# Two cached attention blocks for one token: the order of the loads at both ends of the load queue, the place of the turning, and the bank of the second block's output sums

## The chip, the cores and the metric

The kernel runs on one core of a Trainium2 chip. The metric is the device time in microseconds of one execution; the time given for a kernel is the median of its runs. A trace of one profiled execution gives the durations, the waits and the transfers that are used below.

## The reference

Two independent blocks, A and B, each decode one token for two batch entries with 32 heads of width 192 over a cache of 8192 keys. Both have the same shapes here, and every tensor is bf16. The outputs (2, 1, 640) stand side by side.

```python
def _A_ref(x, k_cache, v_cache, wq, wo):           # _B_ref computes the same
    q = (x @ wq).reshape(B, Sq, Hq, Dh).transpose(0, 2, 1, 3)
    scores = jnp.einsum("bhqd,bhkd->bhqk", q, k) * (Dh ** -0.5)
    p = softmax(scores, axis=-1)
    o = jnp.einsum("bhqk,bhkd->bhqd", p, v)
    return o.transpose(0, 2, 1, 3).reshape(B, Sq, Hq * Dh) @ wo
out = jnp.concatenate([A, B], axis=-1)
```

x is (2, 1, 640), each cache (2, 32, 8192, 192), wq (640, 6144), wo (6144, 640). The caches are 805 of the 837 MB that are read.

## The kernel before, in words

**Units.** The work on the caches is cut into 64 units: a unit is one batch entry of a pair of heads (two batch entries, 16 pairs a block, two blocks). Units 0 to 31 are block A, 32 to 63 block B. "K63" is the K of unit 63, "V61" the V of unit 61. A unit's K or V is one load of 6.29 MB: the two heads lie on the two halves of the 128 partitions, with 128 keys of 192 numbers on each partition.

**One unit on the engines.** VectorE multiplies K by the unit's q, 32 keys a time (`dve_mul`, L280, four products a unit). TensorE sums each product over the 192 numbers by 12 matmuls with the identity (`pe_sum`, L352) into one of the four PSUM banks `scps`, and VectorE reduces the rest (`dve_red`, L283). The maximum goes over the partitions by POOL (L261), ScalarE makes the exponentials (`act_exp`, L317) and writes them into `pb`, the weights of the next matmuls. TensorE adds up their sum (`pe_l`, L358) and multiplies them with V (`pe_pv`, L365: 64 matmuls of 384 columns, two keys a partition in each). In `pb` each matmul has 34 columns: rows 0 and 1 of the result take the first of the two keys, rows 32 and 33 the second, and the 30 columns between are zero. VectorE and ScalarE add the two, divide by the sum and put the head's output into `qall` (L294 to L303).

**Start.** wq of both blocks is loaded whole; q is made by 80 matmuls a block (`pe_q`, L344), over an x that is spread over columns (`xbc`). The two wqs, x and `xbc` lie in `big`, the same SBUF tile that later holds the three buffers for K and V (`BUFE` each, 24576 numbers a partition) and two buffers for products. wq of A lies over buffers 0 and 1, x and `xbc` at the start of buffer 2, wq of B over the rest.

**End.** When all pairs of a block are done, the turning (`pe_turn`, L374, four matmuls a pair) brings the heads' outputs onto the partitions in the bank `oTps`, ScalarE copies them (`act_ot`, L324), and 96 matmuls a block multiply them with wo (`pe_out`, L387) and add into the bank `outps`. ScalarE evicts that (`act_out`, L327) and the output is stored. wo (7.86 MB a block) comes in eight pieces: A in two halves, B in pieces of 16, 16, 8, 4, 2 and 2 of its 48 rows. A row of wo here is 640 numbers on each of 128 partitions.

**Order.** All loads of wq, K, V and wo are issued by SP, in the order in which they are written (the loop of L468 and the one behind it), and each may carry a wait that holds everything behind it on SP. The loads of K and V are K0, K1, V0, K2, V1, and so on to K62, V61, K63, V62, V63; load i takes buffer i mod 3 and waits until load i - 3 has been used: a K by its last product, a V by its matmuls. In place of that, K0 and K1 wait for block A's q and V0 for block B's. wo piece 0 stands ahead of V63 and waits for K63's last product; the other pieces stand behind V63, which is loaded in three cuts.

On the engines each stream is put together from a table of slots, a slot a unit, sorted by an order number within the slot (`put`). In slot u TensorE does the sums of unit u, then the exponentials' sum and the V matmuls of unit u - 1. Slots 64 and 65 (`E1`, `E2`) hold the end: block A's turning, V63's matmuls, A's outputs, block B's turning, B's outputs. TensorE's stream runs as a loop over six slots wherever the slots look alike (`_find`), and is written out elsewhere.

The lines that matter most:

```python
    wq_off = [0, NBUF * BUFE + 2 * PRODE - WQE]
...
    loads = [("k", 0)]
    for u in range(1, NU):
        loads += [("k", u), ("v", u - 1)]
    loads.append(("v", LASTU))
...
        if i < 2:
            w = [("pq", PPB - 1)]
        elif i == 2:
            w = [("pq", NP - 1)]
        if (kind, u) == ("v", LASTU):
            S_sp.add(ld_wo(0), waits=pieces[0][4])
```

Of the kernel before, what the change touches and what calls it, by code (L numbers as in the profile page):

```python
# [6 lines left out]
ACTF = mybir.ActivationFunctionType  # L7
AXL = mybir.AxisListType
BF16 = mybir.dt.bfloat16
# [94 lines left out]
def build_kernel(nc, blocks, out):  # L104
# [4 lines left out]
    T = Sk // 64  # L109
# [12 lines left out]
    scale = float(Dh) ** -0.5  # L122
    NBUF = 3
    MP = 34
    QW = 2 * Dh
    BUFE = T * Dh
    PRODE = TC * Dh
# [3 lines left out]
    with ExitStack() as es:  # L131
# [34 lines left out]
        xoff = 2 * BUFE  # L166
        assert wq_off[0] + WQE <= xoff
        XBE = NBLK * DC * 128
        assert xoff + XBE + D <= wq_off[1]
        xbc = big[:, xoff:xoff + XBE].rearrange("p (k c m) -> p k c m", k=NBLK, c=DC)  # L170
        x4 = big[0:NBLK * B, xoff + XBE:xoff + XBE + D]

        reg = {}
        S_sp = _Stream("sp", sem("s_sp"), reg)
# [30 lines left out]
        bk, b62, b63 = buf["k", LASTU], buf["v", LASTU - 1], buf["v", LASTU]  # L205
        assert (bk, b62, b63) == (2, 0, 1)
        HWR = WR // 2
        woA = bk * BUFE
        pieces = [
            (0, 0, HWR, woA, [("m", LASTU, NCH - 1)]),  # L210
            (0, HWR, WR, woA + HWR * D, [("s", LASTU, NCH - 1)]),
            (1, 0, 16, b62 * BUFE, [("pv", LASTU - 1)]),
            (1, 16, 32, b62 * BUFE + 16 * D, []),
            (1, 32, 40, b63 * BUFE, [("pv", LASTU, 0)]),
            (1, 40, 44, b63 * BUFE + 8 * D, []),
            (1, 44, 46, b63 * BUFE + 12 * D, []),
            (1, 46, 48, b63 * BUFE + 14 * D, []),
        ]
        assert 16 * D <= BUFE // 2 and 32 * D <= BUFE and woA + WR * D <= NBUF * BUFE + 2 * PRODE
        for n in range(len(pieces)):  # L220
            dsem(("wo", n))

# [90 lines left out]
        def act_exp(u):  # L313
            def fn(eng):
                for s in range(2):
                    r = slice(64 * s, 64 * s + 64)
                    ins = eng.activation(pb[u % 2][r, :, s::32], sc[u % 2][r, :].rearrange("p (j a) -> p j a", a=2),  # L317
                                         ACTF.Exp, bias=nb[u % 2][r, :], scale=scale, accum_out=rs[u % 2][r, s:s + 1])
                return ins
            return fn  # L320
# [3 lines left out]
            return lambda eng: eng.activation(oTz[blk][:, :, 2:4], src, ACTF.Identity)  # L324

        def act_out(blk):
            return lambda eng: eng.activation(out_sb[blk][:], outps[0:4, 0:NH2], ACTF.Identity)  # L327

        def out_dma(blk, half):
            dst = out[:, 0, blk * D + half * NH2: blk * D + (half + 1) * NH2]  # L330
# [26 lines left out]
        def pe_l(u):  # L357
            return lambda eng: eng.matmul(ops[u % 2][0:2, QW:QW + 1], rs[u % 2][:], ones[:], start=True, stop=True)  # L358

        def pe_pv(u, j0, j1):  # L360
            vv = kv[buf["v", u]].rearrange("p (j a) d -> p j (a d)", a=2)

            def fn(eng):
                for j in range(j0, j1):
                    ins = eng.matmul(ops[u % 2][0:MP, 0:QW], pb[u % 2][:, j, :], vv[:, j, :],  # L365
                                     start=(j == 0), stop=(j == TJ - 1))
                return ins
            return fn
# [11 lines left out]
        def pe_out(n):  # L380
            blk, r0, r1, off, _ = pieces[n]
            wo = big[:, off:off + (r1 - r0) * D].rearrange("p (i n) -> p i n", n=D)

            def fn(eng):
                for i in range(r0, r1):
                    for half in range(2):
                        ins = eng.matmul(outps[0:4, 0:NH2], oTz[blk][:, i, 2 - 2 * half:6 - 2 * half],  # L387
                                         wo[:, i - r0, half * NH2:(half + 1) * NH2],
                                         start=(i == 0 and half == 0), stop=(i == WR - 1 and half == 1))
                return ins  # L390
            return fn
# [19 lines left out]
        for u in range(NU):  # L411
            for c in range(NCH):
                w = [("k", u), ("qa", u // B), ("qx", u // B), back("s", u, c, 2)]
                if u == 0:
                    w.append(("pq", NP - 1))
                put("dve", u, 2 + 2 * c, dve_mul(u, c), w, ("m", u, c))
                put("dve", u, 2 + 2 * min(c + 1, NCH - 1) + 1, dve_red(u, c),
                    [("s", u, c), key("mx", u - 2), key("exp", u - 2)], ("r", u, c))
                put("pe", u, 0, pe_sum(c),
                    [("m", u, c), back("r", u, c, NCH), ("id1",), ("qx", NP - 1), ("qa", NP - 1)], ("s", u, c), ("s", c))  # L420
            put("dve", u, 12, dve_max(u), [("r", u, NCH - 1), key("ar", u - 2), ("init",)], ("mx", u))
            put("pool", u, 0, pool_ar(u), [("mx", u), key("nb", u - 2)], ("ar", u))
            put("act", u, 0, act_nb(u), [("ar", u), key("exp", u - 2)], ("nb", u))
            put("act", u, 1, act_exp(u), [("nb", u), key("pv", u - 2), key("l", u - 2), ("init",)], ("exp", u))
            w0 = [("exp", u), key("os", u - 2), key("rc", u - 2), ("init",)]
            put("pe", u + 1, 2, pe_l(u), w0, ("l", u), ("l", u % 2))
            cuts = VCUT.get(u)
            if cuts is None:
                put("pe", u + 1, 3, pe_pv(u, 0, TJ), [("v", u)], ("pv", u), ("pv", u % 2, buf["v", u]))
            else:  # L430
                for c, (t0, t1) in enumerate(zip(cuts[:-1], cuts[1:])):
                    put("pe", u + 1, 3 + 0.01 * c, pe_pv(u, t0 // 2, t1 // 2), [("v", u, c)],
                        ("pv", u) if t1 == T else ("pv", u, c))
# [6 lines left out]
        for blk, slot, order in ((0, E1, 0), (1, E2, 0)):  # L440
            for hp in range(PPB * blk, PPB * (blk + 1)):
                lastp = hp == NP - 1
                put("pe", slot if not lastp else E2, order if not lastp else 5, pe_turn(hp),
                    [("of", B * hp + 1), ("place",)] + ([("ot", 0)] if blk else []), ("t", hp))
        put("act", E1, 2, act_ot(0), [("t", PPB - 1), ("init",)], ("ot", 0))
        put("act", E2, 8, act_ot(1), [("t", NP - 1), ("init",)], ("ot", 1))
        where = {0: (E1, 4), 1: (E2, 4)}
        for n, p in enumerate(pieces):
            slot, order = where.get(n, (E2, 6 + 0.01 * n))
            w = [("wo", n), ("ot", p[0])]  # L450
            if p[0] and n == 2:
                w.append(("oev", 0))
            put("pe", slot, order, pe_out(n), w, ("f", n))
# [121 lines left out]
```

## Time and profile before

| | before |
|---|---|
| median of three runs | 1964.46 us |
| the three runs | 1961.86, 1964.46, 1965.69 us |
| profiled execution, its own time | 1963.75 us |
| span of its trace, first to last instruction | 1962.0 us |
| granted TensorE clock, mean | 0.949 |
| busy: TensorE, VectorE, ScalarE, POOL | 78%, 57%, 8%, 2% |
| read from HBM | 836.77 MB |

The trace gives times in microseconds from the first instruction. PE is TensorE's matmuls, PEld its weight loads, DVE VectorE, ACT ScalarE, SPq the instructions by which SP issues loads. A row of the timeline has its start, its duration, the engine, the line of the kernel, the operation, its tiles and their shapes, how many were merged, and in brackets the idle time before it with what ended that. A row of the windows has the stretch, its length, then the busy time of PE, PEld, DVE, ACT and POOL with the number of instructions, the granted clock, the busy share of the 16 DMA engines and GB/s. A row of the loads has the tensor, the queue, the count, the size of one and the microseconds from its issue to its landing. A row of the chain of waits has its start, its duration and what it was. A matmul's own duration counts from its entry to its modelled end; neighbours overlap.

### The profile page before, as it was taken

The page shows a single profiled execution, that of the slowest core. Times are in us where ns is not written, and L with a number is a line of the kernel's source. Part 1 is how long each engine was busy: PE and PEld are TensorE (multiplying, and loading weights), DVE is VectorE, ACT ScalarE, POOL GpSimd, SP SyncE. Part 2 cuts the span into 40 slices and gives each one's busy share as a digit, 9 for nine tenths or more (in the row PEclk, how much of TensorE's full clock was granted, in tenths as well). Part 3 has the DMA queues.
Part 4 walks back from the last instruction along what each step waited for, and adds up shares of the span by engine and source line. Part 5 has one row for each costly group of instructions (what it writes and reads, how often), then busy time and mean ns, then how long its engine had stood idle before and what let it go on. Part 6 is the DMA issues. An engine that isn't in the chain of part 4 may idle for free.

```text
span 1962.0 us, 17861 instructions
## 1 busy us (share of the span) xinstructions
PE 1527.6 (78%) x7781; PEld 744.5 (38%) x7781; DVE 1123.5 (57%) x901; ACT 160.3 (8%) x519; POOL 31.3 (2%) x80
## 2 busy tenths in 40 slices
PE   4787877877877787777787787787787787777888
PEld 2343433333333333333333343343343343333345
DVE  3865565565565565566556556556556556556540
ACT  3100000000000000000000000000000000000000
POOL 1000000000000000000000000000000000000000
PEclk9999999999999988999998999999999898999899
DMA  9999999999999999999999999999999999999977
GB/s 396 433 433 432 433 432 432 433 433 433 431 433 433 433 433 433 433 433 433 433 432 433 432 433 433 432 433 433 433 434 433 433 433 433 433 433 432 433 332 327
DMA packets 20212, 837.12 MB, mean 427 GB/s; under 512 B 2252, under 2 KB 2264, under 8 KB 2648
## 3 DMA queue, kind: packets, MB, share of 16 engines
q1 hardware_dynamic: 20164, 836.77, 98.9%
q8 instruction: 13, 0.21, 0.0%
q14 instruction: 15, 0.12, 0.0%
q10 hardware_dynamic: 20, 0.01, 0.0%
HBM read 836.77 MB, written 0.01 MB: 426 GB/s over the span
## 4 chain that ended last, share of the span: by engine, by line
DMA 49%; PE 30%; DVE 20%; issue 0%; ACT 0%; SPq 0%
DMA big<-in_B_k_cache_dram 24%; DMA big<-in_A_k_cache_dram 22%; DVE big L280 17%; PE ops L365 17%; PE scps L352 11%; DVE sc L283 2%; DMA big<-in_B_wq_dram 2%; PE outps L387 1%; DMA big<-in_B_v_cache_dram 1%; PE scps L344 1%; PE ops L358 0%; PE oTps L374 0%; ACT out_sb L327 0%; SPq L235 0%; DVE mp L289 0%
## 5 line engine op out<-in xcount | busy, mean ns | idle before, releaser
L280 DVE TENSOR_TENSOR big<-big,qall 128x6144 bf16<-128x6144 bf16 x256 | 852.7, 3351 | 534.3 <-DMA big<-in_B_k_cache_dram 277.4
L352 PE MATMUL scps<-big,ident 128*128 128x512 bf16 x3072 | 782.2, 412 | 402.1 <-DVE big L280 402.1
L365 PE MATMUL ops<-big,pb 128*34 128x384 bf16 x4096 | 678.5, 327 | 3.7 <-DMA big<-in_B_v_cache_dram 3.7
L352 PEld LDWEIGHTS scps<-big,ident 128*128 128x128 bf16 x3072 | 304.0, 104 | 873.7 <-DVE big L280 497.8
L365 PEld LDWEIGHTS ops<-big,pb 128*34 128x34 bf16 x4096 | 396.0, 98 | 263.6 <-DMA big<-in_B_v_cache_dram 3.8
L283 DVE TENSOR_REDUCE sc<-scps 128x32 f32<-128x512 f32 x256 | 175.9, 687 | 206.6 <-PE scps L352 206.6
L309 ACT ACTIVATE nb<-mg 64x1 f32<-64x1 f32 x128 | 25.7, 201 | 1705.0 <-POOL mg L261 1704.3
L317 ACT ACTIVATE pb<-sc,nb 64x128 bf16<-64x128 f32 x128 | 81.7, 638 | 3.1
L261 POOL PARTITION_ALL_REDUCE mg<-mp x64 | 25.9, 405 | 1860.4 <-DVE mp L289 1860.4
L344 PE MATMUL scps<-big 128*128 128x384 bf16 x160 | 31.1, 364 | 14.5 <-DMA big<-in_A_wq_dram 11.0
L317 ACT ACTIVATION_READ_ACCUMULATOR pb<-sc,nb 64x1 f32 x128 | 38.5, 301 | 0.0
L289 DVE TENSOR_REDUCE mp<-sc 64x1 f32<-64x128 f32 x128 | 35.9, 280 | 3.1
L270 DVE CAST qall<-scps 64x192 bf16<-64x192 f32 x64 | 22.7, 355 | 19.5 <-PE scps L344 16.8
L303 ACT ACTIVATE qall<-o_sum,rc 2x192 bf16<-2x192 f32 x64 | 29.0, 454 | 18.1 <-DVE o_sum L300 16.4
L344 PEld LDWEIGHTS scps<-big 128*128 128x128 bf16 x160 | 17.1, 108 | 28.2 <-DMA big<-in_A_wq_dram 11.1
L387 PE MATMUL outps<-big,oTz 128*4 128x320 bf16 x192 | 26.6, 299 | 0.7 <-ACT out_sb L327 0.7
L294 DVE RECIPROCAL rc<-ops 2x1 f32<-2x1 f32 x64 | 10.0, 156 | 28.3 <-PE ops L365 26.3
L274 ACT ACTIVATE qall<-scps 64x192 bf16<-64x192 f32 x64 | 20.8, 325 | 34.4 <-DVE qall L270 32.2
L297 DVE COPY o_hi<-ops 2x192 f32<-2x192 f32 x64 | 22.3, 349 | 2.0
L300 DVE TENSOR_TENSOR o_sum<-ops,o_hi 2x192 f32<-2x192 f32 x64 | 22.1, 346 | 2.2
L387 PEld LDWEIGHTS outps<-big,oTz 128*4 128x4 bf16 x192 | 16.1, 85 | 10.7 <-issue 1.2
L358 PEld LDWEIGHTS ops<-ones,rs 128*2 128x2 f32 x128 | 5.5, 82 | 26.8 <-issue 26.7
(24 smaller groups left out, 42.0 us busy)
## 6 DMA issues: line engine op xcount, KB each, us to landing
big<-in_A_k_cache_dram SPq DMA_DIRECT2D x32, 6144.0 KB, 29.2
big<-in_A_v_cache_dram SPq DMA_DIRECT2D x32, 6144.0 KB, 28.1
big<-in_B_k_cache_dram SPq DMA_DIRECT2D x32, 6144.0 KB, 29.1
big<-in_B_v_cache_dram SPq DMA_DIRECT2D x31, 6144.0 KB, 27.9
big<-in_A_wq_dram SPq DMA_DIRECT2D x1, 7680.0 KB, 21.7
big<-in_B_wq_dram SPq DMA_DIRECT2D x1, 7680.0 KB, 39.8
big<-in_A_wo_dram SPq DMA_DIRECT2D x2, 3840.0 KB, 23.3
big<-in_B_wo_dram SPq DMA_DIRECT2D x2, 2560.0 KB, 32.1
```

The costliest lines, as they stand in the source:

```text
L261: return lambda eng: eng.partition_all_reduce(mg[u % 2][:], mp[u % 2][:], 128, bass.bass_isa.ReduceOp.max)
L270: return lambda eng: eng.tensor_copy(qall[ro, B * hp + 1 - s, :], qps[hp % NCH][ri, s * Dh:(s + 1) * Dh])
L280: return lambda eng: eng.tensor_tensor(prod[c % 2], t[:, c * TC:(c + 1) * TC, :], q, ALU.mult)
L283: return lambda eng: eng.tensor_reduce(sc[u % 2][:, c * TC:(c + 1) * TC], scps[c][:], AXL.X, ALU.add)
L289: ins = eng.tensor_reduce(mp[u % 2][r, s:s + 1], sc[u % 2][r, :], AXL.X, ALU.max)
L303: return lambda eng: eng.activation(qall[0:2, u, :], o_sum[:], ACTF.Identity, scale=rc[u % 2][:])
L309: ins = eng.activation(nb[u % 2][r, :], mg[u % 2][r, s:s + 1], ACTF.Identity, scale=-scale)
L317: ins = eng.activation(pb[u % 2][r, :, s::32], sc[u % 2][r, :].rearrange("p (j a) -> p j a", a=2), ACTF.Exp, bias=nb[u % 2][r, :], scale=s ...
L344: ins = eng.matmul(qps[hp % NCH][:, 0:QW], xbc[:, blk, c, :], wq_t[blk][:, c, off:off + QW], start=(c == 0), stop=(c == DC - 1))
L352: ins = eng.matmul(scps[c][:], ident[:], prod[c % 2][:, :, j * DG:(j + 1) * DG], start=(j == 0), stop=(j == NJ - 1))
L365: ins = eng.matmul(ops[u % 2][0:MP, 0:QW], pb[u % 2][:, j, :], vv[:, j, :], start=(j == 0), stop=(j == TJ - 1))
L387: ins = eng.matmul(outps[0:4, 0:NH2], oTz[blk][:, i, 2 - 2 * half:6 - 2 * half], wo[:, i - r0, half * NH2:(half + 1) * NH2], start=(i == 0 ...
```

## The change

- wq of both blocks moves out of buffer 0 (to `BUFE` and behind it), and x and `xbc` get tiles of their own. K0 waits for nothing and stands behind the two wqs; K1 still waits for block A's q, V0 for block B's.
- The 34 columns of each V matmul's weights become a window over a dense row of exponentials (`pb` is 256 numbers a partition in place of 64 x 34). The columns between are no longer zero; the result's rows between hold products that nobody reads. ScalarE writes with a step of two numbers and reads the scores in another order.
- K63 goes ahead of V61: the last loads are K62, K63, V61, V62, V63. On TensorE V61's matmuls (and the sum of its exponentials) move from slot 62 to slot 63, ahead of V62's.
- All wo pieces stand behind V63, ten of them: A in 28 and 20 rows, B in 13, 10, 8 (over V62's buffer) and 6, 4, 3, 2, 2 (over V63's first half). V63 is loaded in two cuts instead of three.
- Block A's turning and its copy move to slot 61, the turning of block B's pairs 16 to 29 to slot 62, that of pair 30 to slot 63; pair 31 stays in slot 65, behind wo piece 0.
- Block B's outputs add up in `scps[0]` and wait only for that bank's last reduction, in place of A's eviction from `outps`.

```diff
-        pb = [sb(f"pb{i}", [128, TJ, MP], BF16) for i in range(2)]
+        pb = [sb(f"pb{i}", [128, 2 * T], BF16) for i in range(2)]
+        xbc = sb("xbc", [128, NBLK, DC, 128], BF16)
+        x4 = sb("x4", [NBLK * B, D], BF16)
...
+        oacc = [outps[:], scps[0][:].rearrange("p a b -> p (a b)")]
...
-        wq_off = [0, NBUF * BUFE + 2 * PRODE - WQE]
+        wq_off = [BUFE, BUFE + WQE]
...
-        VCUT = {LASTU: [0, T // 2, 3 * T // 4, T]}
+        VCUT = {LASTU: [0, T // 2, T]}
...
         loads.append(("v", LASTU))
+        loads[-4], loads[-3] = loads[-3], loads[-4]
...
+        A0 = 28
+        pieces = [(0, 0, A0, woA, [("pv", LASTU - 2), ("s", LASTU, NCH - 1)]), (0, A0, WR, woA + A0 * D, [])]
+        r = 0
+        for n in (13, 10, 8):
+            pieces.append((1, r, r + n, wo0 + r * D, [("pv", LASTU - 1)]))
+            r += n
+        R0 = r
+        for n in (6, 4, 3, 2, 2):
+            pieces.append((1, r, r + n, wo1 + (r - R0) * D, [("pv", LASTU, 0)]))
+            r += n
...
-                    ins = eng.activation(pb[u % 2][r, :, s::32], sc[u % 2][r, :].rearrange("p (j a) -> p j a", a=2),
+                    dst = pb[u % 2][r, :].rearrange("p (g a j s) -> p g a j s", a=2, j=JB, s=2)[:, :, :, :, s]
+                    ins = eng.activation(dst, sc[u % 2][r, :].rearrange("p (g j a) -> p g a j", j=JB, a=2),
...
-                    ins = eng.matmul(ops[u % 2][0:MP, 0:QW], pb[u % 2][:, j, :], vv[:, j, :],
+                    j0s = 4 * JB * (j // JB) + 2 * (j % JB)
+                    ins = eng.matmul(ops[u % 2][0:MP, 0:QW], pb[u % 2][:, j0s:j0s + MP], vv[:, j, :],
...
-                        ins = eng.matmul(outps[0:4, 0:NH2], oTz[blk][:, i, 2 - 2 * half:6 - 2 * half],
+                        ins = eng.matmul(oacc[blk][0:4, 0:NH2], oTz[blk][:, i, 2 - 2 * half:6 - 2 * half],
...
-            put("pe", u + 1, 2, pe_l(u), w0, ("l", u), ("l", u % 2))
+            pslot = u + 2 if u == LASTU - 2 else u + 1
+            put("pe", pslot, 2, pe_l(u), w0, ("l", u), ("l", u % 2))
...
+        for hp in range(NP):
+            blk = hp // PPB
+            slot, order = (NU - 3, 5) if blk == 0 else (NU - 2, 5) if hp < NP - 2 else (NU - 1, 5) if hp < NP - 1 else (E2, 1)
+            put("pe", slot, order, pe_turn(hp),
+                [("of", B * hp + 1), ("place",)] + ([("ot", 0)] if blk else []), ("t", hp))
+        put("act", NU - 3, 6, act_ot(0), [("t", PPB - 1), ("init",)], ("ot", 0))
+        put("act", E2, 6, act_ot(1), [("t", NP - 1), ("init",)], ("ot", 1))
         for n, p in enumerate(pieces):
             w = [("wo", n), ("ot", p[0])]
+            if p[0]:
+                w.append(("r", LASTU, 0))
+            put("pe", E2, 0.01 * n if n == 0 else 2 + 0.01 * n, pe_out(n), w, ("f", n))
...
-            if i < 2:
-                w = [("pq", PPB - 1)]
-            elif i == 2:
-                w = [("pq", NP - 1)]
-            if (kind, u) == ("v", LASTU):
-                S_sp.add(ld_wo(0), waits=pieces[0][4])
+            if i in (1, 2):
+                w = [("pq", PPB * i - 1)]
...
-        for n in range(1, len(pieces)):
+        for n in range(len(pieces)):
             S_sp.add(ld_wo(n), waits=pieces[n][4])
```

More of the change, by code (lines that the diff above doesn't have):

```diff
@@ L124, in build_kernel @@
     MP = 34
+    JB = 16
     QW = 2 * Dh
@@ L163, in build_kernel @@
         WQE = DC * Hn * Dh
-        wq_off = [0, NBUF * BUFE + 2 * PRODE - WQE]
+        wq_off = [BUFE, BUFE + WQE]
+        assert BUFE + 2 * WQE == NBUF * BUFE + 2 * PRODE
         wq_t = [big[:, o:o + WQE].rearrange("p (c n) -> p c n", c=DC) for o in wq_off]
[L166 to L171, printed above, removed]
         reg = {}
@@ L203, in build_kernel @@
                 reg[(kind, u)] = (bsem[i % NBUF], 16 * bcount[i % NBUF])
-        bk, b62, b63 = buf["k", LASTU], buf["v", LASTU - 1], buf["v", LASTU]
+        bk, b62, b63 = buf["v", LASTU - 2], buf["v", LASTU - 1], buf["v", LASTU]
         assert (bk, b62, b63) == (2, 0, 1)
[L207 to L219, printed above, removed]
+        woA, wo0, wo1 = bk * BUFE, b62 * BUFE, b63 * BUFE
+        A0 = 28
[8 more added lines that the diff above has]
+            r += n
+        assert r == WR and R0 * D <= BUFE and (WR - R0) * D <= BUFE // 2 and woA + WR * D <= NBUF * BUFE + 2 * PRODE
         for n in range(len(pieces)):
@@ L326, in act_out @@
         def act_out(blk):
-            return lambda eng: eng.activation(out_sb[blk][:], outps[0:4, 0:NH2], ACTF.Identity)
+            return lambda eng: eng.activation(out_sb[blk][:], oacc[blk][0:4, 0:NH2], ACTF.Identity)
         def out_dma(blk, half):
@@ L425, in build_kernel @@
             w0 = [("exp", u), key("os", u - 2), key("rc", u - 2), ("init",)]
-            put("pe", u + 1, 2, pe_l(u), w0, ("l", u), ("l", u % 2))
+            pslot = u + 2 if u == LASTU - 2 else u + 1
+            put("pe", pslot, 2, pe_l(u), w0, ("l", u), ("l", u % 2))
             cuts = VCUT.get(u)
             if cuts is None:
-                put("pe", u + 1, 3, pe_pv(u, 0, TJ), [("v", u)], ("pv", u), ("pv", u % 2, buf["v", u]))
+                put("pe", pslot, 3, pe_pv(u, 0, TJ), [("v", u)], ("pv", u), ("pv", u % 2, buf["v", u]))
             else:
                 for c, (t0, t1) in enumerate(zip(cuts[:-1], cuts[1:])):
-                    put("pe", u + 1, 3 + 0.01 * c, pe_pv(u, t0 // 2, t1 // 2), [("v", u, c)],
+                    put("pe", pslot, 3 + 0.01 * c, pe_pv(u, t0 // 2, t1 // 2), [("v", u, c)],
                         ("pv", u) if t1 == T else ("pv", u, c))
@@ L439, in build_kernel @@
         E1, E2 = NU, NU + 1
[L440 to L447, printed above, removed]
+        for hp in range(NP):
[5 more added lines that the diff above has]
+        put("act", E2, 6, act_ot(1), [("t", NP - 1), ("init",)], ("ot", 1))
         for n, p in enumerate(pieces):
-            slot, order = where.get(n, (E2, 6 + 0.01 * n))
             w = [("wo", n), ("ot", p[0])]
-            if p[0] and n == 2:
-                w.append(("oev", 0))
-            put("pe", slot, order, pe_out(n), w, ("f", n))
+            if p[0]:
+                w.append(("r", LASTU, 0))
+            put("pe", E2, 0.01 * n if n == 0 else 2 + 0.01 * n, pe_out(n), w, ("f", n))
         for blk, n in ((0, 1), (1, len(pieces) - 1)):
```

## The prediction

> **What bounds the kernel now.** I read the page first (busy shares, the 40 slices, the queue), then the windows at both ends, then the chain of waits and the timeline of the last 110 us.
>
> ```profile
> span 1962.0 us, 17861 instructions
> GB/s 396 433 433 432 433 432 432 433 433 433 431 433 433 433 433 433 433 433 433 433 432 433 432 433 433 432 433 433 433 434 433 433 433 433 433 433 432 433 332 327
> q8 instruction: 13, 0.21, 0.0%
> q1 hardware_dynamic: 20164, 836.77, 98.9%
> L352 PE MATMUL scps<-big,ident 128*128 128x512 bf16 x3072 | 782.2, 412 | 402.1 <-DVE big L280 402.1
> L365 PE MATMUL ops<-big,pb 128*34 128x384 bf16 x4096 | 678.5, 327 | 3.7 <-DMA big<-in_B_v_cache_dram 3.7
> ...
> L317 ACT ACTIVATE pb<-sc,nb 64x128 bf16<-64x128 f32 x128 | 81.7, 638 | 3.1
> ```
>
> The one load queue is busy 98.9% of the span and moves 433 GB/s in every slice but the first (396) and the last two (332, 327). A unit is one K and one V, 2 x 6.29 MB, so 29.06 us at 433 GB/s; TensorE needs (782.2 + 678.5) / 64 = 22.8 us of it. The middle can't be shortened without moving fewer bytes, and the change moves the same bytes. Only the two ends can give time.
>
> ```profile
> 36.00:46.00 10.00, 6.55 (x26) 3.19 (x25) 3.54 (x10) 3.88 (x12) 0.00 (x0) 0.71 0.90 340
> 1884.00:1900.00 16.00, 13.54 (x48) 5.12 (x48) 11.88 (x7) 0.00 (x0) 0.00 (x0) 0.81 0.33 123
> 1900.00:1950.00 50.00, 45.57 (x384) 28.76 (x383) 3.81 (x12) 3.73 (x12) 0.35 (x1) 0.93 1.00 425
> 60.00:1880.00 1820.00, 1426.27 (x7112) 686.98 (x7113) 1075.39 (x813) 133.67 (x439) 25.58 (x63) 0.95 1.00 433
> ```
>
> The last column is GB/s. From 36 to 46 us, 340 instead of 433 means 10 x 93 / 433 = 2.1 us of stream lost; from 1884 to 1900, 123 means 16 x 310 / 433 = 11.5 us. After 1950 nothing is left to load.
>
> ```profile
> 1880.84 3.37 DVE big L280
> ...
> 1897.81 19.63 DMA big<-in_B_v_cache_dram
> ...
> 1917.49 12.21 PE ops L365 x64
> ...
> 1936.31 2.65 PE oTps L374 x60
> ...
> 1946.59 13.21 PE outps L387 x96
> ...
> 1959.82 0.43 ACT out_sb L327
> ```
>
> So the last 80 us are one chain: K63's products, whose end lets the queue go on (wo piece 0 waits for it, and V63 stands behind that piece on SP), V63's landing, its 64 matmuls, then 192 output matmuls with the turning between them. The wo pieces have landed long before TensorE has used them.
>
> **Part 1, K0 without a wait.**
>
> ```profile
> 37.65 0.80 SPq L235 DMA_DIRECT2D big<-in_A_k_cache_dram  x2
> ...
> 41.06 16.05 PE L344 MATMUL scps<-big 128*128 128x384 bf16 x80 [3.45 <-DMA big<-in_B_wq_dram]
> ```
> ```profile
> 1.25 39.77 DMA big<-in_B_wq_dram
> ```
> ```profile
> big<-in_A_k_cache_dram SPq DMA_DIRECT2D x1, 6144.0 KB, 20.1
> ...
> big<-in_A_k_cache_dram SPq DMA_DIRECT2D x1, 6144.0 KB, 34.3
> ```
>
> K0 and K1 wait for block A's q (37.65). The second wq lands at 1.25 + 39.77 = 41.0, K0 at 37.65 + 20.1 = 57.7, 16.7 later; K1 at 38.02 + 34.3 = 72.3, 14.5 later. Queued early, K0 should also need 14.5: **-2.1** (windows 2.1, landings 2.2). Bounds: 2.2 and 0. Nothing takes it back: K1 still waits for A's q (37.65, needed by 52, which is 3.7 ahead of K0's new landing, a lead worked out below), V0 for B's q (41.06 + 16.05 = 57.1, needed by 66), and every load behind moves up.
>
> **Part 2, the end.** All times are on the axis of before; the 2.1 comes off last. In steady running the loads keep their places, so K63 lands where V61 did and V61 where K63 did.
>
> ```profile
> 1839.31 0.33 SPq L235 DMA_DIRECT2D big<-in_B_v_cache_dram  x1
> 1851.77 6.63 DVE L280 TENSOR_TENSOR big<-big,qall 128x6144 bf16<-128x6144 bf16 x2 [7.38 <-DMA big<-in_B_k_cache_dram]
> 1855.18 7.04 PE L352 MATMUL scps<-big,ident 128*128 128x512 bf16 x24 [2.45 <-DVE big L280]
> 1864.15 3.35 DVE L280 TENSOR_TENSOR big<-big,qall 128x6144 bf16<-128x6144 bf16 x1
> 1867.52 0.33 SPq L235 DMA_DIRECT2D big<-in_B_v_cache_dram  x1
> 1872.26 0.35 DVE L300 TENSOR_TENSOR o_sum<-ops,o_hi 2x192 f32<-2x192 f32 x1
> 1894.06 3.35 DVE L280 TENSOR_TENSOR big<-big,qall 128x6144 bf16<-128x6144 bf16 x1
> 1897.44 0.33 SPq L235 DMA_DIRECT2D big<-in_A_wo_dram  x1
> 1897.47 2.76 PE L352 MATMUL scps<-big,ident 128*128 128x512 bf16 x12 [1.10 <-DVE big L280]
> 1900.28 10.58 PE L365 MATMUL ops<-big,pb 128*34 128x384 bf16 x64
> ...
> 1297.63 6.63 DVE L280 TENSOR_TENSOR big<-big,qall 128x6144 bf16<-128x6144 bf16 x2 [8.23 <-DMA big<-in_B_k_cache_dram]
> ...
> 1308.65 3.35 DVE L280 TENSOR_TENSOR big<-big,qall 128x6144 bf16<-128x6144 bf16 x1
> ```
> ```profile
> big<-in_B_v_cache_dram SPq DMA_DIRECT2D x1, 6144.0 KB, 27.0
> ...
> big<-in_B_v_cache_dram SPq DMA_DIRECT2D x1, 6144.0 KB, 27.8
> ...
> big<-in_A_wo_dram SPq DMA_DIRECT2D x1, 3840.0 KB, 12.8
> ```
>
> K63 is there at 1839.31 + 27.0 = 1866.3, before VectorE has finished K62. Four products of a K take from 14.4 us (1297.63 to 1312.0, TensorE at speed) over 15.7 (K62, 1851.77 to 1867.5) to 16.6 (K63 before, 1880.84 to 1897.4); VectorE ends the unit 5.1 later (1867.5 to 1872.6). So K63's products now start at 1871.3 to 1872.6 and end at 1885.7 to 1889.2. I take 1887.3, because A's 64 turns now run between V60's matmuls and K62's first sums, where TensorE waited 2.45 us, while the gap before K63's sums stays. The last sums end 2.8 later: 1890.1.
>
> ```profile
> 1856.00:1859.40 3.40, 3.40 (x10) 0.50 1.00 434
> ```
>
> What spreads 14.4 to 16.6 is this granted clock of 0.50 behind a gap of 2.45 us. [...]
>
> From 1890.1 TensorE has no gap: three units of V (61, 62, 63) at 10.6 each, 31.7; four turns (2.65 per 60) and the single-column matmuls between, some 0.4; 192 output matmuls at 13.2 per 96, 26.4; the last four turns, 0.3. That ends at 1948.9, and the way to the end of the span stays 1962.0 - 1959.8 = 2.2: **1951.1**. What this takes off the end: the wait for V63 (3.7), 120 turns (2.65 per 60, so 5.3, moved to where TensorE waits anyway), block B's wait for A's eviction (it sums in another bank), and most of the hole.
>
> **What must hold for it.** V62 lands at 1867.52 + 27.8 = 1895.3. An empty queue paid 12.8 - 3.93 MB / 0.433 = 3.7 us over the moving (wo piece 0), so V63 must be issued by 1891.6; its wait is K63's last product, 1887.3 (1889.2 at the latest). V63 then lands at 1909.8, wo piece 0 needs V61's matmuls (1900.9, wanted by 1906.1), the first B pieces V62's (1911.5, wanted by 1924.6), the last ones V63's first half (1917, wanted by 1936). All ten pieces are 15.73 MB, 37.0 us at 425: the last lands near 1946.9, the stream's own limit. TensorE reaches that piece at 1948.4, and piece 0 (landed 1920.6) at 1922.2. On SP only loads stand behind these waits.
>
> **What costs nothing.** The probabilities are scattered with another stride, reading every other score: 0.64 us each now, not shown in the new form, half to double that. A steady unit's two are used one K later; unit 63's now wait for V61's matmuls and still have V62's 10.6 us ahead of their use; without that cover 1.3 us. V matmuls take 34 filled columns where 30 were zero: same instruction, same size, 0 (but see the slow rival). Smaller memsets and x in its own tiles: ahead of wq's landing, 0. B's separate bank: 0. The loop on TensorE ends a period of six units earlier, since units 61 and 62 no longer look alike; some six packets of instructions of 16 KB more (the 13 that moved are 0.21 MB) at 433 / 16 = 27 GB/s for one of the 16 DMA engines are 0.6 us each: 3.6 if one engine gets all, 0.2 if they spread. I take **+0.3**. One load more behind V62 (12 for 11) is nothing: the last two landed 0.8 us apart, which is their bytes.
>
> ```profile
> big<-in_B_wo_dram SPq DMA_DIRECT2D x1, 320.0 KB, 26.4
> ...
> big<-in_B_wo_dram SPq DMA_DIRECT2D x1, 320.0 KB, 26.7
> ```
>
> **The sum.** 1951.1 - 2.1 + 0.3 = 1949.3, 12.7 less than the span of 1962.0. The profiled execution took 1963.75 (1.75 lie outside the span); it would be 1951.1. The median of the runs, 1964.46, is 0.7 above it: **1951.8**.
>
> **Rivals.**
> - *The stream ends last.* If K62 and K63 take 14.4 each, TensorE waits for the last piece: 1946.9 + 0.6 for four matmuls, + 2.2 - 2.1 + 0.3 = 1947.9, or 1950.4 as a median. [...] For it: the steady units at 14.4; against it: the row of 0.50 above.
> - *The start pays nothing.* K0's first packets may be slow wherever they stand, or K63's products come so late that V63 is held up by a like amount: 1953.9. For it: the 340 GB/s hold whatever the first packets of a K cost by themselves; against it: K1, queued behind K0, landed 14.5 after it.
> - *Slower: filled weights slow the V matmuls.* With 34 live columns the granted clock could fall in L365's stretches. The end now has 192 of them in a row, so from 12.7 / 192 = 66 ns each (165 now) the kernel is slower than before; at half clock a unit needs 12.2 + 21.2 = 33.4 us of TensorE where the stream gives 29.06, and 64 x 4.3 more make about 2230. Against it: the q matmuls (L344) fill 128 columns and run 80 in 16.05 us.
> - *Slower: K0 takes turns with wq.* Were the queued loads served in turn, both wqs would land with K0 near 55, A's q come 16 us behind at 71, and the stream stand still for those 16 us from 55 on: 1951.8 + 2.1 + 16 = 1970. Against it: A's q was done at 37.65, before the second wq had landed at 41.0; in turn, the two wqs would have landed together.
>
> **How the numbers follow.** Forecast 0.60 (1950.4 to 1953.7 by its own bounds), the stream last 0.17, the start for nothing 0.14, filled weights 0.04, turns 0.03, no change because several of these eat it 0.02. The three runs spread by 3.8 us, so 0.2%, 3.9 us, is about what can be told from no change. Faster 0.91, same 0.02, slower 0.07. The range 1948.0 to 1956.5 takes in the first three cases with that spread, and leaves out the rest.
>
> **What would show it.** K0 landing 14.5 after the second wq; the stream at 433 from 36 to 46 and no hole after V62; K63's products starting straight behind K62's unit; TensorE without a gap from the last sums to the last output matmul, and 2.2 us behind it; the granted clock 1.0 in the V matmuls. I am wrong if the second wq lands later than 41, if the queue runs dry before V63, if V matmuls take over 165 ns at full clock, or if TensorE waits for wo pieces by more than a microsecond.

## The result, and the profile after

| | before | after |
|---|---|---|
| median | 1965.08 us (4 runs, 1961.86 to 1965.95) | 1952.37 us (4 runs, 1950.65 to 1954.36) |
| ratio | | 0.9942, 95% interval 0.9929 to 0.9955 |
| profiled execution, span of its trace | 1963.75, 1962.0 us | 1952.38, 1950.6 us |

The change takes 0.6% off. The forecast was 1951.8 us, with a span of 1949.3. The page of the changed kernel:

```profile
span 1950.6 us, 17823 instructions
...
GB/s 415 433 423 433 433 434 434 432 430 431 433 435 433 434 431 430 433 434 434 434 433 430 432 433 433 434 435 429 433 431 435 433 434 431 432 431 433 433 413 338
...
q1 hardware_dynamic: 20308, 836.77, 99.5%
q8 instruction: 18, 0.29, 0.1%
...
L366 PE MATMUL ops<-big,pb 128*34 128x384 bf16 x4096 | 676.6, 326 | 0.0
...
L317 ACT ACTIVATE pb<-sc,nb 64x128 bf16<-64x128 f32 x128 | 55.8, 436 | 11.4 <-PE ops L366 8.5
```

The same bytes come at the same 433 GB/s; the first slice has 415 in place of 396, the last but one 413 in place of 332. TensorE waits for no V any more (0.0 us of idle time in the row of L366). Its windows (stretch, length, busy times, clock, DMA share, GB/s):

```profile
36.00:46.00 10.00, 6.68 (x27) 3.20 (x26) 3.80 (x11) 3.96 (x13) 0.00 (x0) 0.71 0.95 411
1884.00:1900.00 16.00, 14.90 (x88) 7.99 (x87) 4.91 (x5) 0.40 (x2) 0.35 (x1) 1.00 0.92 376
...
1941.00:1946.00 5.00, 5.00 (x39) 3.15 (x37) 0.00 (x0) 0.00 (x0) 0.00 (x0) 1.00 0.10 37
```

In the stretch of the hole behind V62 (1884 to 1900) 376 GB/s come where 123 came. From 1941 to 1946 some 37 GB/s come: of 16 DMA engines at 433 / 16 = 27 each, little more than one is still at work. The end of the chain of waits of the changed kernel:

```profile
1851.11 6.63 DVE big L279 x2
...
1862.20 3.28 DVE big L279
...
1870.58 3.27 DVE big L279
1873.85 0.05 issue
1873.90 5.31 PE scps L352 x12
...
1883.79 3.28 DVE big L279
1887.07 0.05 issue
1887.11 2.76 PE scps L352 x12
...
1890.05 20.91 PE ops L366 x128
...
1911.34 10.51 PE ops L366 x64
1921.85 7.70 PE outps L388 x56
...
1935.34 13.05 PE scps L388 x96
```

K63's products now follow K62's unit at once, and from 1887.1 on there is only TensorE. From K62's landing (1851.1; 1851.8 before) to the end of the span it is 99.5 us, where it was 110.2: 10.7 of the 11.4 us between the two spans come from the end.

### The profile page after: what moved, and what is told of

It reads as the page before. It is cut to its first block, busy times and chain, and to the rows that moved or that the text cites. A ratio compares the mean times of both kernels' runs of the same rounds, so it can differ in the third digit from the quotient of the medians.

```text
span 1950.6 us, 17823 instructions
## 1 busy us (share of the span) xinstructions
PE 1536.1 (79%) x7781; PEld 747.1 (38%) x7781; DVE 1121.0 (57%) x901; ACT 142.3 (7%) x519; POOL 28.0 (1%) x80
## 3 DMA queue, kind: packets, MB, share of 16 engines
q1 hardware_dynamic: 20308, 836.77, 99.5%
## 4 chain that ended last, share of the span: by engine, by line
DMA 47%; PE 32%; DVE 20%; issue 0%; ACT 0%; SPq 0%
DMA big<-in_B_k_cache_dram 24%; DMA big<-in_A_k_cache_dram 21%; PE ops L366 18%; DVE big L279 18%; PE scps L352 12%; DVE sc L282 2%; DMA big<-in_B_wq_dram 2%; PE scps L344 1%; PE outps L388 1%; PE scps L388 1%; PE ops L358 0%; DVE mp L288 0%; PE oTps L375 0%; ACT out_sb L327 0%; DVE qall L269 0%
## 5 line engine op out<-in xcount | busy, mean ns | idle before, releaser
L352 PE MATMUL scps<-big,ident 128*128 128x512 bf16 x3072 | 793.1, 417 | 386.2 <-DVE big L279 386.1
L366 PE MATMUL ops<-big,pb 128*34 128x384 bf16 x4096 | 676.6, 326 | 0.0
L366 PEld LDWEIGHTS ops<-big,pb 128*34 128x34 bf16 x4096 | 395.6, 98 | 258.8
L317 ACT ACTIVATE pb<-sc,nb 64x128 bf16<-64x128 f32 x128 | 55.8, 436 | 11.4 <-PE ops L366 8.5
L260 POOL PARTITION_ALL_REDUCE mg<-mp x64 | 25.8, 404 | 1852.6 <-DVE mp L288 1852.6
L344 PE MATMUL scps<-big,xbc 128*128 128x384 bf16 x160 | 30.8, 361 | 14.2 <-DMA big<-in_A_wq_dram 10.9
L344 PEld LDWEIGHTS scps<-big,xbc 128*128 128x128 bf16 x160 | 17.0, 107 | 27.7 <-DMA big<-in_A_wq_dram 10.9
L317 ACT ACTIVATION_READ_ACCUMULATOR pb<-sc,nb 64x1 f32 x128 | 23.7, 185 | 0.0
L388 PE MATMUL outps<-big,oTz 128*4 128x320 bf16 x96 | 13.4, 299 | 0.0
L388 PE MATMUL scps<-big,oTz 128*4 128x320 bf16 x96 | 13.2, 299 | 0.0
```

What stands on the lines that cost most here:

```text
L260: return lambda eng: eng.partition_all_reduce(mg[u % 2][:], mp[u % 2][:], 128, bass.bass_isa.ReduceOp.max)
L317: ins = eng.activation(dst, sc[u % 2][r, :].rearrange("p (g j a) -> p g a j", j=JB, a=2), ACTF.Exp, bias=nb[u % 2][r, :], scale=scale, acc ...
L344: ins = eng.matmul(qps[hp % NCH][:, 0:QW], xbc[:, blk, c, :], wq_t[blk][:, c, off:off + QW], start=(c == 0), stop=(c == DC - 1))
L352: ins = eng.matmul(scps[c][:], ident[:], prod[c % 2][:, :, j * DG:(j + 1) * DG], start=(j == 0), stop=(j == NJ - 1))
L366: ins = eng.matmul(ops[u % 2][0:MP, 0:QW], pb[u % 2][:, j0s:j0s + MP], vv[:, j, :], start=(j == 0), stop=(j == TJ - 1))
L388: ins = eng.matmul(oacc[blk][0:4, 0:NH2], oTz[blk][:, i, 2 - 2 * half:6 - 2 * half], wo[:, i - r0, half * NH2:(half + 1) * NH2], start=(i ...
```

## The experiments

Two theories stood against each other throughout: the end is TensorE's own chain, so that everything on that chain counts and nothing else; or the end is set by the stream of loads. The times from K62's landing to the end are used beside the medians, since runs of one kernel spread by up to 4 us.

**V61 ahead of K63 again.**

```diff
-        loads[-4], loads[-3] = loads[-3], loads[-4]
...
-        bk, b62, b63 = buf["v", LASTU - 2], buf["v", LASTU - 1], buf["v", LASTU]
+        bk, b62, b63 = buf["k", LASTU], buf["v", LASTU - 1], buf["v", LASTU]
...
-        pieces = [(0, 0, A0, woA, [("pv", LASTU - 2), ("s", LASTU, NCH - 1)]), ...
+        pieces = [(0, 0, A0, woA, [("m", LASTU, NCH - 1), ("s", LASTU, NCH - 1)]), ...
...
-            pslot = u + 2 if u == LASTU - 2 else u + 1
+            pslot = u + 1
```

> The changed kernel with V61 ahead of K63 again; everything else of the change is kept (wo piece 0 waits for K63's last product and last sums in place of V61's matmuls). Theory: moving K63 forward brought next to nothing, because V61's matmuls went behind K63's sums with it. From K62's landing to the end of the span the changed kernel takes 99.5 us; here K63 lands 29.1 after K62, its products take 14.4 to 16.6, the sums 2.8, then two units of V (21.1) and 26.8 of turning and outputs, 2.2 to the end: 96.4 to 98.6, or 97.8 where the last wo piece binds. So 0 to 2 us faster than the change, about 1951. Rival (the early K63 is what closes the hole): the queue runs dry behind V62 again and the kernel is 5 us or more slower than the change, 1957 or more.

1950.77 us, span 1949.2: 1.6 less than the change by the medians, 1.4 by the spans. The timeline of this kernel (start, duration, engine, line, operation, tiles, count, idle before):

```profile
1880.39 6.62 DVE L278 TENSOR_TENSOR big<-big,qall 128x6144 bf16<-128x6144 bf16 x2 [8.34 <-DMA big<-in_B_k_cache_dram]
...
1891.40 3.35 DVE L278 TENSOR_TENSOR big<-big,qall 128x6144 bf16<-128x6144 bf16 x1
...
1920.15 7.77 PE L387 MATMUL outps<-big,oTz 128*4 128x320 bf16 x56 [1.06 <-DMA big<-in_A_wo_dram]
...
1933.55 13.38 PE L387 MATMUL scps<-big,oTz 128*4 128x320 bf16 x96
```

K63 lands where it did before, 9.9 us later than its products start in the change, and still nothing is lost: V61's matmuls now fill the wait for K63, and only two units of V are left behind its sums in place of three. Its products take 14.4 us here (1880.39 to 1894.75) for 16.6 in the change, but the second trace below shows that this is not what counts. TensorE even waits 1.06 us for wo piece 0. The windows of this kernel show no hole without the early K63:

```profile
1884.00:1900.00 16.00, 13.29 (x65) 5.83 (x64) 13.45 (x12) 0.57 (x3) 0.35 (x1) 1.00 0.98 418
```

So the early K63 closed nothing: V63 is issued at 1880.4 here, behind V61's matmuls, and at 1887.1 in the change, behind K63's last product. A second comparison, with the change beside it on one chip:

> The changed kernel itself, beside the next one on one chip. 1952 to 1953, span 1950 to 1951.5; its last output matmul ends 2 to 2.5 us behind the landing of the last wo piece.

> The changed kernel with V61 ahead of K63 again, beside the change on one chip. Theory: 1.0 to 1.6 us faster than the change, because its K63 meets TensorE at speed and the last output matmul follows the last wo piece within 0.8 us. Rival: within 0.5 us of it, the first comparison being chance.

1951.91 us for the change (five runs, 1951.31 to 1954.30), 1950.59 for the old order (five runs, 1950.23 to 1950.93): 1.3 less, and no run of the one reaches the other. Against the kernel before, the ratios are 0.9939 (0.9925 to 0.9953) and 0.9930 (0.9917 to 0.9944). This is the fastest version found. The reason that the expectation gave is not borne out: in this second trace of the old order K63's products took 15.5 us, with half the clock from 1882.9 to 1886.3, and in that of the change 15.7. From the start of K62's products to the end of the span it is 97.9 us in both traces of the old order, with 14.4 us as with 15.5, and 99.5 and 100.3 in those of the change. The last output matmul follows the last wo piece by 0.8 us in the old order, as expected, and by 3.1 us in the second trace of the change, which is more than the 2 to 2.5 expected. So the end of the old order hangs on the last wo piece, which in the first trace was issued at 1915.72 and landed 30.5 us later:

```profile
big<-in_B_wo_dram SPq DMA_DIRECT2D x1, 320.0 KB, 30.5
```

That is 1946.2, and the span ends 3.0 behind it; in the change the last piece lands at 1946.0 and the span ends 4.6 behind it.

**wo piece 0 ahead of V63 again**, on top of the old order.

```diff
-        pieces = [(0, 0, A0, woA, [("m", LASTU, NCH - 1), ("s", LASTU, NCH - 1)]), (0, A0, WR, woA + A0 * D, [])]
+        pieces = [(0, 0, A0, woA, [("m", LASTU, NCH - 1)]), (0, A0, WR, woA + A0 * D, [("s", LASTU, NCH - 1)])]
...
+            if (kind, u) == ("v", LASTU):
+                S_sp.add(ld_wo(0), waits=pieces[0][4])
...
-        for n in range(len(pieces)):
+        for n in range(1, len(pieces)):
```

> V61 ahead of K63, and wo piece 0 (28 rows of A) ahead of V63 on SP again, waiting for K63's last product, as in the kernel before; turning, banks, the start and the other pieces as in the change. Theory: the hole in the stream is what cost most. Piece 0 and V63 are issued near 1895 instead of V63 at 1879, the queue stands for some 4 us on its last engine and more on the others, all later loads land about 6 us later, V63's second half near 1921, and TensorE starts V63's matmuls 3 to 8 us late: 4 to 8 us slower than the kernel with the old order alone, 1955 to 1959. Rival (TensorE's own chain sets the end whatever the queue does): within 1 us of the old order alone.

1960.44 us, span 1958.5: 9.7 more than the old order alone by the medians, 9.3 by the spans, which is above the 4 to 8 that were expected. A window and TensorE's timeline of this kernel:

```profile
1884.00:1900.00 16.00, 13.29 (x66) 5.82 (x64) 13.30 (x12) 0.72 (x4) 0.36 (x1) 1.00 0.43 166
```
```profile
1897.46 10.57 PE L365 MATMUL ops<-big,pb 128*34 128x384 bf16 x64
1917.05 6.90 PE L365 MATMUL ops<-big,pb 128*34 128x384 bf16 x32 [8.62 <-DMA big<-in_B_v_cache_dram]
1924.36 5.38 PE L365 MATMUL ops<-big,pb 128*34 128x384 bf16 x32 [0.41 <-DMA big<-in_B_v_cache_dram]
```

The hole is back (166 GB/s for 418), and TensorE waits 8.6 + 0.4 us for V63. Two things stand in V63's way here: the stall, and the 4.59 MB of piece 0 ahead of it, 10.6 us at 433 GB/s. The expectation had priced the second too low. V63's halves land at 1917.0 and 1924.3 here, 14.8 us later than with the old order alone (1902.2 and 1909.5). Less the 10.6 us of bytes, that leaves some 4.2 us for the stall. With those 4.2 alone V63 would have come before TensorE was ready for it (1906.4 for 1908.5), and only the last wo piece, on which the end of the old order hangs, would have come later. The bytes alone would have kept TensorE waiting for at least 4.3 us (1912.8 for 1908.5). This split is an estimate from the two traces; no run has the one without the other.

**The turning late again.**

```diff
-            slot, order = (NU - 3, 5) if blk == 0 else (NU - 2, 5) if hp < NP - 2 else (NU - 1, 5) if hp < NP - 1 else (E2, 1)
+            slot, order = (E1, 0) if blk == 0 else (E2, -1) if hp < NP - 1 else (E2, 1)
-        put("act", NU - 3, 6, act_ot(0), ...
+        put("act", E1, 2, act_ot(0), ...
```

> The changed kernel with A's 64 turns back behind V62's matmuls and B's 60 back behind V63's. Theory: the end is a chain on TensorE without a gap, so 2.9 and 2.7 us of turning go onto it whole, less the pair that already stood there: 5.3 us slower than the change, about 1957.7, span 1955.9. Rival (the end is set by the stream's last landing): at most 3 us slower, because TensorE would only use up what it waits for the pieces.

1958.11 us, span 1956.3: 5.7 more than the change, by the medians and by the spans. From the last sums to the end of the span it takes 65.9 us, in the change 60.7: 5.2 more. From the chain of waits of this kernel:

```profile
1890.57 20.91 PE ops L366 x128
1911.48 2.82 PE oTps L375 x64
...
1914.42 10.51 PE ops L366 x64
1924.92 2.65 PE oTps L375 x60
```

The turns stand on the chain with their whole length, while the stream's last piece lands no later than in the change (1945.95 for 1946.04). In the change TensorE's chain is the end.

**Block B in the bank of A again** (`oacc = [outps[:], outps[:]]`, waiting for `("oev", 0)`).

> The changed kernel with block B's outputs in the bank of A's again, so that B's first piece waits for A's eviction. Theory: TensorE's chain gets that wait and nothing else, 0.7 us (0.74 in the kernel before): 1953.1, span 1951.3. Rival (the stream's last piece sets the end): no difference.

1953.49 us, span 1951.7. From the last sums (1890.24) to the end of the span it takes 61.5 us, in the change (1889.87) 60.7: the 0.7 that were expected. The medians alone, 1.1 apart, could not have told it.

**K0 waits again** (`if i < 3: w = [("pq", PPB * max(i, 1) - 1)]`).

> The changed kernel, but K0 waits for block A's q again, as K1 does. Theory as predicted: K0 lands 16.7 us behind the second wq in place of 15.5 and everything moves by what the last of the 16 engines loses there: about 1 us slower than the change, 1953.4 (2.1 us, 1954.5, if the whole stretch counts as the prediction had it). Rival (the start is hidden): no difference, because the lag of the slowest engine later swallows it; then K62 lands at 1851.1 as in the change.

1952.94 us, ratio 0.9939 (0.9922 to 0.9955), against 0.9942 for the change. K0's landing in the change (issued at 1.72) and here (issued at 39.01), each from the list of loads of its own trace:

```profile
big<-in_A_k_cache_dram SPq DMA_DIRECT2D x1, 6144.0 KB, 55.0
```
```profile
big<-in_A_k_cache_dram SPq DMA_DIRECT2D x1, 6144.0 KB, 18.9
```

So K0 lands at 56.7 in the change and at 57.9 with the wait, and K62's products start at 1851.11 and here at

```profile
1851.12 3.36 DVE L279 TENSOR_TENSOR big<-big,qall 128x6144 bf16<-128x6144 bf16 x1 [9.60 <-DMA big<-in_B_k_cache_dram]
```

The lead of 1.2 us is gone by the end. The other traces agree: in the eleven with the early K0 and an undisturbed stream, K62's products start between 1850.86 and 1851.55, and 1851.12 with the wait lies among them. Between the trace of the change and this one the lead goes up and down in steps of 0.6 to 1.2 us, at single loads: in both kernels a load now and then lands about 15.5 us behind the one ahead of it, where 14.53 is the median of the trace of the change. In the change seven loads up to K62 do so. Each lands 5 to 7 us behind an instruction packet of 8 KB in queue q14 (the load of 1792.9 behind the packet of 1786.0), and each time the last of the load's 16 parts falls about 1 us further behind the others. Five more such packets between 500 and 1440 us delayed no load. So a link in time is shown, and not the cause.

**Half the units with the old weights**, 34 columns with 30 zeros, in even units alone.

> The changed kernel with the old form of the V weights (34 columns each, 30 of them zero, written in steps of 34 and 32) for even units and the new form for odd ones; both do not fit in the memory with x in its own tiles. Theory: V matmuls take the same 165 ns in both forms, the exponentials 638 ns in even units and 436 in odd ones, the span stays within 1.5 us of 1950.6. Rival (filled weights cost clock or time): odd units' V matmuls are slower than even ones, or the granted clock falls in them.

One run of 1953.5 us, span 1951.8. The page's groups of this kernel:

```profile
L372 PE MATMUL ops<-big,pb 128*34 128x384 bf16 x4096 | 676.6, 326 | 0.0
...
L322 ACT ACTIVATE pb<-sc,nb 64x128 bf16<-64x128 f32 x128 | 68.8, 537 | 11.5 <-PE ops L372 8.5
```

The V matmuls take what they took, each of the 4096 between 325 and 339 ns, and 537 ns is the mean of 638 and 436: the new form makes an exponential 0.2 us shorter, and nobody waits for it.

**TensorE kept busy ahead of K63's sums.** 48 matmuls of the identity with itself behind the turning in slot 62.

> The changed kernel with 48 more matmuls (identity by identity, 128 columns, into the bank of A's outputs before it is first used, 2.6 us) behind the turning in slot 62, in the gap of 3.1 us ahead of K63's first sums. Theory: the 16.6 us that K63's products take in the changed kernel are 14.4 plus the granted clock of 0.50 behind that gap; without the gap they take 14.4, the chain ends 2.2 us earlier, and the last wo piece (landing 1946.0, four matmuls, 2.2 us) then sets the end: 1.5 to 2 us faster, span near 1948.9. Rival (VectorE sets the 16.6 by itself): no change, K63's products take 16.6 again.

1952.76 us, span 1951.2: the gain did not come. K63's products did get shorter, from 16.6 to 15.1 us (1872.54 to 1887.68), but K62's took 16.6 where the first trace of the change had 14.4. The added matmuls stand behind K62's sums and can't have done that; the second trace of the change, without them, has 16.0 and 15.7 us. TensorE's windows ahead of and in K62's sums of this kernel (PE's busy time, clock, DMA share, GB/s):

```profile
1850.10:1853.50 3.40, 3.40 (x65) 0.99 1.00 434
1853.50:1860.30 6.80, 6.55 (x24) 0.50 1.04 443
```

TensorE was busy for the whole first stretch, and the clock halved all the same. All but 0.9 us of that stretch were turns, matmuls whose weights have 2 rows. In the second trace of the change too, 3.40 us of 3.40 busy with the end of K62's sums and then turns (1868.6 to 1872.0) are followed by 6.8 us at half clock. That made a new theory: such matmuls do not count for the clock. Three kernels asked for it, with more matmuls behind each V.

```diff
+        for s in range(2, NU - 3):
+            put("pe", s, 6, pe_fill, [("place",)], ("fill", s), "fill")     # ("id1",) with full rows
```

> The changed kernel with 56 more matmuls behind the V matmuls of every unit from slot 2 to 60, of the turning's form (weights of 2 rows x 128, 96 columns; 2.5 us, into the bank that A's outputs use later). It fills the gap ahead of each K's first sums. Theory: matmuls of two rows do not keep the clock up, so the mean granted clock stays near 0.943 and halves about once a unit as now. Rival (any matmul counts): no half clock left in the middle, mean 0.99 or more. The stream sets the time either way: 1950 to 1953.

One run of 1964.2 us, span 1962.5, outside the 1950 to 1953 that were expected; so slowed, its mean clock of 0.937 answers nothing. The page has

```profile
q8 instruction: 103, 1.69, 0.4%
```

in place of 18 packets: the loop of six slots had grown from 226 to 338 TensorE instructions a slot, and between 310 and 1720 us the instruction queue q8 moves 80 packets here and none in the change. Five times TensorE stood ahead of its sums, 7.2 us at most and 34.3 in all, with nothing in the profile to wait for; the change has no such idle time of its matmuls. With fewer and longer matmuls the loop stays small:

> The changed kernel with 12 more matmuls behind the V matmuls of every unit from slot 2 to 60: weights of 2 rows x 128, 512 columns, 2.6 us, into the bank that A's outputs use later. They are few, so that TensorE's loop grows little. Theory: two rows do not keep the clock up; in the middle the granted clock halves in as many units as without them (46 half stretches between 130 and 1800 us in the change). Rival (any matmul counts): under 15 half stretches there. The span stays within 2 us of 1950.6 either way.

> The same 12 matmuls at the same place, with weights of 128 rows x 128 (the identity). Theory: these do count, so the gap ahead of each K's sums is gone, under 15 half stretches are left between 130 and 1800 us, the mean granted clock is 0.98 or more, and four products of a K take 14.4 us in nearly all units. The span stays within 2 us of 1950.6, since the stream sets the middle. Rival (what is spent on turning has nothing to do with the clock, which halves for another reason): as many half stretches as in the change.

One run each, 1953.36 and 1952.84 us, spans 1951.6 and 1951.1. Between 130 and 1800 us the trace has 46 stretches of half clock in the change, 45 with the two rows, 23 with the full rows; mean granted clock of the whole run 0.943, 0.948 and 0.974. The eleven other traces, which have no full rows added, have 41 to 47. The sums' groups of the change, of the two rows and of the full rows:

```profile
L352 PE MATMUL scps<-big,ident 128*128 128x512 bf16 x3072 | 793.1, 417 | 386.2 <-DVE big L279 386.1
```
```profile
L352 PE MATMUL scps<-big,ident 128*128 128x512 bf16 x3072 | 787.9, 415 | 234.5 <-DVE big L279 234.4
```
```profile
L352 PE MATMUL scps<-big,ident 128*128 128x512 bf16 x3072 | 749.1, 398 | 274.9 <-DVE big L279 274.9
```

Two rows fill the gap just as long (234 us of idle time left, the full rows 275) and change nothing in the clock (45 slow stretches for 46); full rows halve their number (23). The 15 or fewer that were expected were not reached, nor the clock of 0.98.

The traces show where the border lay. In the change the stretches of half clock last 3.41 us (37 of them) or twice that (14), so take the clock in windows of that length, between 130 and 1800 us, and in each the time in which TensorE was busy with other than two-row matmuls. In the change the windows ahead of the 46 falls to half clock have at most 1.36 us of it, and the 387 windows that kept the full clock at least 1.41. With the two-row matmuls added to each unit it is at most 1.36 and at least 1.44; if those matmuls are counted in, 37 of the 45 falls follow a window with more than 1.5 us, some with all 3.41. With the full rows added, most of the 23 falls that are left follow 1.43 to 1.45 us, more than the least with which the change kept the full clock (1.41). So the border was some 1.4 us of 3.41 in these three traces, and matmuls of two rows counted for nothing. Two falls near the end, ahead of K63's sums in the first trace of the change and ahead of K62's in the kernel before (the last row has PEld, DVE, ACT and POOL too):

```profile
1869.70:1873.10 3.40, 1.07 (x26) 1.00 1.00 434
1873.10:1879.90 6.80, 6.00 (x15) 0.50 1.03 443
```
```profile
1852.60:1856.00 3.40, 0.95 (x5) 0.41 (x5) 3.40 (x2) 0.00 (x0) 0.00 (x0) 1.00 1.07 463
```

The 1.07 us were turns alone; the 0.95 us were matmuls with weights of 128 rows.

## Why the prediction was right, and where it was off

The span came out at 1950.6 for 1949.3. The 1.3 us are 1.4 at the start and 0.4 at K62 and K63, less 0.3 on the last chain and the 0.3 allowed for packets of instructions. By its own steps:

- **What bounds the end: right.** TensorE has no gap from the last sums (1889.9) to the last output matmul (1948.4): 58.5 us for 58.8. The late turning and the single bank put 5.2 and 0.7 us back, close to the 5.3 and 0.7 of the forecast's rows. The way from there to the end was 2.2, as before.
- **K62 and K63: the range right, K62's reason wrong.** From the start of K62's products to the last sums it took 38.8 us for 38.3. K62 took 14.4, the lower end, and K63 16.6, the upper end. The forecast gave as K62's reason that A's turns fill the gap ahead of its sums. They ran there, but matmuls of two rows, as the turns are, did not keep the clock up (45 half stretches with them added, 46 without), and in the eleven other traces with the turns at this place K62 took 15.3 to 16.6. That it took 14.4 here was luck: by the border above, its gap (1851.1 to 1854.5) fell across two windows (1849.2 to 1852.6 and 1852.6 to 1856.0) with 1.9 and 1.5 us of full-row matmuls. In the second trace of the same kernel it fell into one (1851.6 to 1855.0, 0.6 us) and the clock halved; there K62 took 16.0, K63 15.7, and the whole 39.5, 1.2 more than forecast. K63's 16.6 came with a clock of 0.50 from 1873.1 to 1879.9, behind a window that held turns alone. The forecast laid its row of 0.50 to a gap of 2.45 us; the window ahead of it held 0.95 us of full-row matmuls, under the border.
- **The start: the term that was mis-sized.** The forecast took off 2.1 us and said that nothing takes it back. K0 came 15.5 behind the second wq, not 14.5, and by K62 the kernel was 0.7 us ahead of before, which is no more than K62's spread between traces of kernels with the same start; with K0's wait put back, K62 came at the same time to 0.02 us. The bandwidth of 36 to 46 us did rise from 340 to 411, but in these traces a load's use starts behind the last of its 16 parts: K0's parts land over 2.96 us in the change and over 2.58 before, K62's over 9.2, the last one, at 1851.08, 5.4 behind the fifteenth, and K62's first product starts at 1851.11. The rest of the lead went at the single late loads, whose cause stays open. The rival that the start pays nothing was right on this term, without bringing the time that it was given.
- **The early K63: not what the forecast's sum suggests.** It listed the chain through it rightly, but did not ask what the chain would be without it. That is 1.3 to 1.6 us shorter by the medians: what K63 gains by coming 14.5 us earlier, V61's matmuls lose by standing behind it.
- **Costs at nothing: right** for the weights, the exponentials and the cuts. Five more packets of instructions came (18 for 13), as the shorter loop let expect; their 0.3 us could not be told apart.
- **The rivals.** The stream did not end last in the change (its last piece landed 2.3 us ahead of the last matmul), but it does in the old order. Filled weights cost no clock: the three last units of V ran at 1.0 (no half clock from 1879.9 to the end of the span), and a V matmul took 326 ns on average for 327 before. The queue served the loads in order: the second wq landed at 41.2, K0, issued 0.5 us behind it, at 56.7.

## What to carry to other kernels

Where a tail is a chain on one engine, price each part by putting it back alone: here the turning (5.2 us) and the place of the wo loads (9.3 us on top of the old order) carried the gain, and the reordering that looked cleverest cost 1.3 to 1.6. Such prices need not add up to the whole: in the kernel before, 2.9 us of turns filled part of the wait for V63. Loading a tile earlier gains nothing where its work only changes places with other work on the same engine (K63, 14.5 us earlier). A load was used here only behind the last of its parts (K62's came 5.4 us behind the fifteenth), so time won in mean bandwidth at the start need not arrive at the end. K62's gap, behind 1.9 and 1.5 us of full-row matmuls in two windows, left the clock at 1.0 in one trace of the change, and behind 0.6 us in one window halved it in the other, so one trace of one unit is no proof; compare several.

## What the hardware showed beside that

- Matmuls with weights of two rows did not keep TensorE's clock up: 3.40 us busy out of 3.40, 2.5 of them with such matmuls, were followed by 6.8 us at 0.50. With full rows added there were 23 half stretches for 46. The border was some 1.4 us of full-row matmuls in a window of 3.41 us (at most 1.36 ahead of a fall in the change, at least 1.41 where the clock stayed).
- A loop of six slots with 226 instructions of TensorE each ran with no packet in the instruction queue q8 from 310 to 1720 us; with 338 each there were 80 in that stretch and 103 of 16 KB in all, and the one run was 12 us longer by the span.
- An exponential of 64 x 128 took 638 ns before, when its results went out in steps of 32 and 34 numbers, 436 ns in the change with steps of two, the order of reading having changed too.
